# A new hand-written order for the VectorE, ScalarE and GpSimd steps and the output steps of a fused convolution, norm and gated FFN kernel

## The chip, the cores and the metric

The kernel runs on one core of a Trainium2 chip. The metric is the device time of one execution in microseconds (us). The kernel before takes 2584.48 us in the median of three runs (2583.52 to 2584.78).

The engines are named as in the profile: PE is TensorE's matmuls and PEld its weight loads, DVE is VectorE, ACT is ScalarE, POOL is GpSimd, and SP (SyncE) is used here for issuing DMAs.

## The reference

Two steps, from x of shape (8, 4096, 192), taken as 32768 tokens of 192 channels:

```python
# 1: causal depthwise convolution, 7 taps, one set of softmaxed taps for each of 8 heads of 24 channels
w = softmax(weight, axis=-1)                      # (8, 7)
y[b, s, c] = sum_k w[c // 24, k] * x_pad[b, s + k, c]      # x_pad: 6 zero rows in front of every batch
# 2: RMS norm and a gated FFN without biases
xn  = y / sqrt(mean(y * y, axis=-1) + 1e-6) * rms_g
g   = xn @ w_gate                                 # (32768, 1536)
val = xn @ w_val                                  # (32768, 1536)
out = (silu(g) * val) @ w_out                     # (32768, 192)
```

All arrays are f32 in DRAM.

## The kernel before, in words

**Pairs.** The 32768 tokens are worked on in 32 pairs of token tiles, a pair being two tiles of 512 tokens. Pair 0 is done plainly in the prologue, while the weights are converted. Pairs 1 to 31 all follow one list, `ORDER`, written out by hand; nothing at build time reorders it. A pair is a product stage and an output stage on TensorE. While TensorE works on pair p, the other engines also prepare pair p + 1 (its x operands), convolve pair p + 2, and finish pair p - 1 (a token of the list that ends in "-" belongs to the pair before).

**Fewer products.** Both matrix products go by a bilinear scheme: sums and differences of blocks of weights are made once, sums and differences of blocks of data in every pair, and then 15 products take the place of a larger number. The price is many elementwise sums, which is why VectorE, ScalarE and GpSimd are busy too.

**Product stage (L840).** The 1536 hidden columns are four units of 384. Each unit has 15 products, and each product is made twice: on the lower 64 rows of the TensorE array for the gate, on the upper 64 rows for the value, so a "round" is one product of each half. That is 4 x 15 x 2 = 120 products of 64x128 by 64x512 in a pair, in an order fixed by `CHAINS`. They land in eight PSUM banks of 512 columns, four for each half. A bank is free again only when another engine has read it, and the next product that takes it waits for that.

**The steps on a unit.** In the list, the first letter is the engine (A ScalarE, V or P or W VectorE, G GpSimd, Q an adding DMA issued by GpSimd's queue, D a DMA on SP's queue), and then comes the step: `AF0.1.0` is ScalarE doing step F0 for half 1 (upper) of unit 0. S copies a bank to a tile in SBUF, F copies a bank into another bank so that two sums can go on from it (L792 on ScalarE, L796 on VectorE), C, D and N (L866, L856, L860) combine a bank with a tile, R is a result (L874; with W it stays in its bank), G is the silu (L886, ScalarE), M multiplies gate and value (L894, VectorE or GpSimd). "p2" in the list means two TensorE steps. So a step's place in the list sets which TensorE steps it stands between, and its place in its own engine's queue; each engine takes its instructions strictly in that order, and the waits between engines come from the data.

**Sums of hidden columns.** From the hidden values (`ht`), sums such as `df`, `de`, `p4`, `ab`, `abe`, `abd`, `bcf` are made for the output stage, per unit: "Gde.2" is such a sum on GpSimd (L1074 for one unit, L1052 for several), "Qde.0" a DMA that adds one block to another in SBUF (L1050, L1072), and "Akp4.2 Pp4.2" a copy of one operand by ScalarE (L746) followed by the sum on VectorE. Units 0 to 3 have indices behind the dot, so "Qbe.0123" adds all four (1 MB), "Qabe.13" two of them (512 KB).

**Output stage (L1029).** 60 steps in the order of `OUTS`; "11.3" is output product 11 for unit 3. A step has four matmuls of 128x32 by 128x256, for four quarters. Each product number needs one of the sums above as its data. The accumulators use halves of PSUM banks, `BANKS` telling which; copies (F, S), joins (D, L1096), transposes (T, L1042) and the stores `st0`, `st1` (L1115, SP) take them to the output. Some of these steps for pair p run at the head of pair p + 1.

**The next pairs.** The convolution is 14 tap steps "cv k_j" per list (L471, L479) into halves of PSUM banks (`SIDE` says which). The norm is a square on ScalarE (`Asq`), a reduction, a power on GpSimd (L529) and a multiplication; `place` writes the result to DRAM (L687), and `fetA`, `fetB` (L703, L706) read it back as x operands. The x sums X0 to X6 and X22 (L738, L727; X22 makes two of them in one instruction) and the exchanges of array halves, `swA` and `swB` (L713, two DMAs each, on SP's queue), complete the operands of the next pair: x blocks are moved from the lower 64 partitions to the upper and back.

```python
nc.gpsimd.dma_start(out=dst, in_=b, accum_op=ALU.add)     # a Q step
```

The last pair has no pair behind it: `last()` puts its output steps in the order `LAST`, with the joins, transposes and stores as early as they can go.

Of the kernel before, what the change touches and what calls it, by code (L numbers as in the profile page):

```python
# [19 lines left out]
def kernel(  # L20
# [14 lines left out]
    H, K = weight.shape  # L35
# [53 lines left out]

    SPAN = 1509  # L90
    PLACE = {'a': 3, 'b': 4, 'c': 5, 'd': 0, 'e': 1, 'f': 2}
    BANKS = {'K': 1, 'R': 0, 'N': 0, 'C01': 0, 'C34': 1}
    OUTS = (
# [3 lines left out]
    )  # L97
    LAST = "7.2 14.2 10.1 13.0 13.2 13.3 13.1 12.0 12.3 12.2 12.1 3.0 0.3 0.0 0.1 0.2 2.0 2.1 2.3 2.2 1.1 1.2 1.3 1.0"
    ORDER = (
# [30 lines left out]
    )  # L130

    cst = ctx.enter_context(tc.tile_pool(name="cst", bufs=1))
# [330 lines left out]
    def part_tap(p, k, j):  # L463
# [4 lines left out]
        if k == 0:  # L468
            h = (SIDE if p > 2 else (0, 1, 0))[j]
            acc[p, j] = h, pick(h, False)  # L470
# [11 lines left out]
        if k == K - 1:  # L482
            h, i = acc.pop((p, j))
            free[h].append(i)
            ended[p] = ended.get(p, 0) + 1
            if ended[p] == len(SIDE):
                x_sb.pop(p)
# [280 lines left out]
    def pick(h, full):  # L768

        i = next((i for i in free[h] if ((h, i) in whole) == full), free[h][0])  # L770
        free[h].remove(i)
        return i
# [5 lines left out]
    def put(at, do):  # L778
        heapq.heappush(line, (at, next(tick), do))
# [148 lines left out]
            )  # L928
            yield

    SIDE = (1, 1, 1)
    regs = held[0 : 2 * NU] + [more[:, i] for i in range(2)]
    REG = {"AB": 0, "CB": 1, "X": 2, "S": 3}

# [26 lines left out]
    def out_steps(p):  # L961
        every, end = " ".join(OUTS).split(), LAST.split()
        return every if p < PAIRS - 1 else every[: -len(end)] + end

    class Pair:
# [29 lines left out]
        def open(self, b, full):  # L995
            b = PART.get(b, (b, 0))[0]
            if b in self.bk:
                return
            h = BANKS[b]
            i = pick(h, full)  # L1000
# [13 lines left out]
        def products(self):  # L1014
# [4 lines left out]
            for w in out_steps(self.p):  # L1019
                n, u = (int(i) for i in w.split("."))  # L1020
                src, b = LEFT[n]
                fresh = b in BANKS and b not in self.bk
                if fresh:
# [335 lines left out]

    for j in range(len(SIDE)):  # L1360
        put(c + 240 + 700 * (j // 2), functools.partial(part_tap, 2, 0, j))
# [152 lines left out]
```

## Time and profile before

| what | value |
|---|---|
| median of three runs | 2584.48 us |
| profiled execution | 2584.59 us, of which the span in the trace is 2582.8 |
| busy: PE, PEld, DVE, ACT, POOL | 99%, 63%, 93%, 76%, 80% of the span |
| granted TensorE clock | 0.999 of full speed |
| DMA | 259.33 MB, 100 GB/s in the mean |
| product stage, output stage of one pair | 52.98 us, 26.04 us |

The page is one profiled execution. Its first part gives for each engine the busy time, the share of the span and the number of instructions. The chain of waits starts from the last instruction and goes back, at each step to what released it, so its shares say what the end hung on. In a timeline, a row is start, duration, engine, line, operation, output and inputs by the program's names with partitions and elements, and in brackets the idle time of the engine before the row and what ended it. In the rows of groups, the number behind x is the count, then come busy time and the mean in ns. The DMA rows give the size of one and the median time from issue to landing.

### The profile page before, as it was taken

To read this page: it belongs to the slowest core of one execution; us is meant where nothing else is said; L and a number is where in the kernel's file an instruction comes from. 1 tells how busy PE (TensorE), PEld (TensorE's weight loads), DVE (VectorE), ACT (ScalarE), POOL (GpSimd) and SP (SyncE) were. 2 spreads that over 40 slices of the span, in tenths; PEclk is the share of its full clock that TensorE was granted. 3 is DMA by queue.
4 is the path that set the end of the run, shared out by engine and by line. 5 is a ranking of instruction groups with operands and counts; after the bars stand their busy time and mean duration, and the time that the engine had idled before them with its cause. 6 is when DMAs were issued, how large, how long until landed. Compare 5 with 4: busy or idle time off the path is not lost.

```text
span 2582.8 us, 61875 instructions
## 1 busy us (share of the span) xinstructions
PE 2568.2 (99%) x23114; PEld 1627.8 (63%) x23114; DVE 2405.7 (93%) x4009; ACT 1957.8 (76%) x3749; POOL 2056.9 (80%) x1581
## 2 busy tenths in 40 slices
PE   8999999999999999999999999999999999999999
PEld 6856666666666666666666666666666555666665
DVE  8799999999999999999999999999999999999976
ACT  6588777787777887777877778777788777787765
POOL 3897777977778877789777788777887777978777
PEclk9999999999999999999999999999999999999999
DMA  6444555445545545554455554455644455544442
GB/s 145 92 87 89 103 102 114 98 95 101 109 96 115 99 86 107 101 116 96 95 101 107 100 113 96 86 111 98 121 92 98 93 109 107 108 95 92 95 99 46
DMA packets 535411, 259.33 MB, mean 100 GB/s; under 512 B 458566, under 2 KB 462278, under 8 KB 531142
## 3 DMA queue, kind: packets, MB, share of 16 engines
q1 hardware_dynamic: 507316, 181.83, 34.7%
q0 software_dynamic: 26288, 73.15, 15.5%
q8 instruction: 182, 2.98, 0.5%
q14 instruction: 119, 0.97, 0.1%
q10 hardware_dynamic: 1506, 0.40, 0.1%
HBM read 100.10 MB, written 49.55 MB: 58 GB/s over the span
## 4 chain that ended last, share of the span: by engine, by line
PE 98%; ACT 1%; DMA 1%; POOL 0%; issue 0%; DVE 0%; SPq 0%; DVEq 0%; POOLq 0%; ACTq 0%
PE ps L840 63%; PE ps L1029 30%; PE ps L1161 2%; PE ps L1202 1%; DMA xa<-xa 0%; ACT early L412 0%; POOL xa L738 0%; DMA x<-in_x_dram 0%; POOL early L1052 0%; POOL early L1074 0%; ACT sq L597 0%; ACT xa L668 0%; PE ps L642 0%; ACT L434 0%; ACT tile L792 0%
## 5 line engine op out<-in xcount | busy, mean ns | idle before, releaser
L840 PE MATMUL ps<-xa,wf 64*128 64x512 f32 x7440 | 1646.4, 592 | 1.6 <-DMA xa<-xa 0.3
L840 PEld LDWEIGHTS ps<-xa,wf 64*128 64x128 f32 x7440 | 1050.0, 186 | 584.5 <-issue 122.8
L792 ACT ACTIVATE tile<-ps 128x512 f32<-128x512 f32 (+1 forms) x770 | 433.4, 570 | 199.5 <-PE ps L1029 108.3
L792 ACT ACTIVATE tls<-ps 128x512 f32<-128x512 f32 (+1 forms) x687 | 386.6, 567 | 167.8 <-PE ps L1029 103.5
L792 ACT ACTIVATE ps<-ps 128x512 f32<-128x512 f32 (+1 forms) x713 | 387.8, 547 | 122.0 <-PE ps L1029 92.0
L894 POOL TENSOR_TENSOR ht<-ht,tile 128x512 f32<-128x512 f32 x305 | 387.8, 1281 | 92.6 <-ACT tile L886 79.1
L1029 PE MATMUL ps<-ht,x 128*32 128x256 f32 x5952 | 390.6, 380 | 0.1
L894 POOL TENSOR_TENSOR ht<-ht,tls 128x512 f32<-128x512 f32 x253 | 321.8, 1279 | 63.6 <-ACT tls L886 55.2
L479 DVE SCALAR_TENSOR_TENSOR ps<-xh,tp,ps 128x512 f32<-128x512 f32 x450 | 322.8, 748 | 1.0 <-DMA xd<-yn 0.9
L1029 PEld LDWEIGHTS ps<-ht,x 128*32 128x32 f32 x5952 | 192.8, 110 | 143.8 <-issue 23.5
L1029 PE MATMUL ps<-early,x 128*32 128x256 f32 x3968 | 254.1, 379 | 0.0
L874 DVE TENSOR_TENSOR tile<-ps,tile 128x512 f32<-128x512 f32 x347 | 236.8, 685 | 15.0 <-ACT tile L792 7.7
L529 POOL TENSOR_TENSOR r<-r,nhalf 128x8 f32<-128x8 f32 x29 | 48.4, 1669 | 241.4 <-ACT r L525 241.4
L874 DVE TENSOR_TENSOR ht<-ps,tile 128x512 f32<-128x512 f32 x325 | 221.6, 685 | 10.4 <-ACT tile L792 6.3
L1052 POOL TENSOR_TENSOR early<-early,ht 128x1024 f32<-128x1024 f32 x93 | 225.9, 2496 | 0.7 <-PE ps L1029 0.2
L886 ACT ACTIVATE tile<-tile 128x512 f32<-128x512 f32 x347 | 215.7, 625 | 1.9
L874 DVE TENSOR_TENSOR tls<-ps,tls 128x512 f32<-128x512 f32 x273 | 185.4, 684 | 9.3 <-ACT tls L792 3.6
L1029 PEld LDWEIGHTS ps<-early,x 128*32 128x32 f32 x3968 | 129.6, 110 | 84.7 <-ACT ps L792 5.1
L886 ACT ACTIVATE tls<-tls 128x512 f32<-128x512 f32 x273 | 168.8, 624 | 1.7
L874 DVE TENSOR_TENSOR ht<-ps,tls 128x512 f32<-128x512 f32 x233 | 159.0, 684 | 6.1 <-ACT tls L792 3.4
L1074 POOL TENSOR_TENSOR early<-ht 128x512 f32<-128x512 f32 x124 | 159.6, 1287 | 2.7
L1029 PE MATMUL ps<-early,wo_sb 128*32 128x256 f32 x2232 | 143.6, 379 | 0.0
(165 smaller groups left out, 3629.1 us busy)
## 6 DMA issues: line engine op xcount, KB each, us to landing
xa<-xd SPq DMA_DIRECT2D x186, 256.0 KB, 4.4
xa<-xa SPq DMA_DIRECT2D x124, 256.0 KB, 4.0
ht<-ht POOLq DMA_DIRECT2D x31, 1024.0 KB, 7.7
xd<-yn SPq DMA_DIRECT2D x248, 96.0 KB, 2.5
out_dram<-o_sb SPq DMA_DIRECT2D x244, 96.0 KB, 2.0
xh<-in_x_dram SPq DMA_DIRECT2D x192, 105.0 KB, 3.7
xa<-xd SPq DMA_DIRECT2D x124, 128.0 KB, 4.8
more<-ht POOLq DMA_DIRECT2D x62, 256.0 KB, 3.3
```

The lines of the kernel that those rows point to most:

```text
L479: nc.vector.scalar_tensor_tensor(out=dst, in0=xk, scalar=w, in1=at, op0=ALU.mult, op1=ALU.add)
L529: nc.gpsimd.tensor_tensor(out=r, in0=r, in1=nhalf[:, 0 : nb * NR], op=ALU.pow)
L792: nc.scalar.activation(out=dst, in_=src, func=AF.Copy, scale=float(s))
L840: nc.tensor.matmul(out=self.new(v, h, True) if first else self.old(v, h), lhsT=wf[self.u][HALF[h], WAT[i], :], rhs=x_op(XOP[i], h), start= ...
L874: nc.vector.tensor_tensor(out=dst, in0=self.old(v, h), in1=t[:], op=plus(s))
L886: nc.scalar.activation(out=t[:], in_=src[:], func=AF.Silu)
L894: engine[eng].tensor_tensor(out=self.hv(v), in0=src, in1=t[:], op=ALU.mult)
L1029: nc.tensor.matmul(out=to[q * Q : (q + 1) * Q, :], lhsT=left[:, u, a], rhs=cols[:, i * HALFT : (i + 1) * HALFT], start=fresh, stop=True, s ...
L1052: nc.gpsimd.tensor_tensor(out=dst, in0=a, in1=b, op=ALU.add)
L1074: engine[eng].tensor_tensor(out=dst, in0=a, in1=b, op=ALU.add)
L1161: nc.tensor.matmul(out=bank(h, bks[h])[:], lhsT=wf[u][HALF[h], AT[h][k] * NF + f, :], rhs=xb[HALF[h], g, k, :], start=(k == 0), stop=(k == ...
L1202: nc.tensor.matmul(out=bank(h, bks[h])[:, w : w + D], lhsT=hts[f // NF][HALF[h], g, f % NF, j * P : (j + 1) * P], rhs=wo_sb[HALF[h], f, :] ...
```

## The change

The list `ORDER` is replaced by another order of nearly the same steps, and `OUTS`, `LAST`, one entry of `BANKS` and two of `SIDE` with it. The 180 TensorE steps of a pair and the number of steps on ScalarE (116), GpSimd (42 sums) and SP (8) in the list are the same; VectorE has one plain step fewer and one W step more (104 V, 15 P and 3 W for 105, 16 and 2), and there are four adding DMAs for five. What differs apart from places:

- copies of banks: `VF0.1.0` becomes `AF0.1.0`; `AF3.1.2` and `AF3.1.3` become `VF3.1.2` and `VF3.1.3`, while `VF3.0.2` and `VF3.0.3` become `AF3.0.2` and `AF3.0.3`
- products of gate and value: `GM2.1.3` becomes `VM2.1.3`, `GM3.1.2` becomes `VM3.1.2`, `VM5.1.3` becomes `GM5.1.3`; results kept in the bank are `WR3.1.2`, `WR2.1.3`, `WR3.1.3` instead of `WR3.1.3`, `WR5.1.3`
- adding DMAs: `Qde.0` and `Qde.1` become one `Qde.01`, `Qabe.13` becomes `Qabe.23` (with a new `Gabe.1` on GpSimd), `Qabd.0` becomes `Qabd.01`; `Qbe.0123` stays
- x sums: GpSimd's `GX5` and the two on VectorE `PX0` and `PX6` with their ScalarE copies become `GX0` and `GX22` on GpSimd
- the square of the norm (`Asq-`) is moved to the front of the pair
- the exchanges: `swA` from behind two TensorE steps of the next pair to four steps before the pair's end, `swB` from four steps before the end to five
- the stores `st0`, `st1` and the fetches `fetA`, `fetB` take other places in SP's queue
- one accumulator (`R`) opens in the other half of its bank, and so do two of the three groups of convolution taps (`SIDE`)

```diff
-    BANKS = {'K': 1, 'R': 0, 'N': 0, 'C01': 0, 'C34': 1}
+    BANKS = {'K': 1, 'R': 1, 'N': 0, 'C01': 0, 'C34': 1}
     OUTS = (
-        "6.2 11.2 6.0 6.1 11.0 11.1 6.3 4.0 11.3 4.1 4.2 9.1 14.0 14.3 14.1 4.3 9.2 9.0 9.3 8.1",
-        "8.3 5.0 5.2 5.1 5.3 8.0 3.1 7.0 8.2 10.2 7.1 10.0 3.3 3.2 10.3 7.3 7.2 14.2 10.1 13.0",
-        "1.1 13.2 1.2 12.0 12.3 12.2 12.1 13.3 13.1 3.0 1.3 1.0 0.3 0.0 0.1 2.0 0.2 2.1 2.3 2.2",
+        "6.0 11.1 11.2 4.0 6.3 11.0 6.2 6.1 11.3 4.2 4.1 14.2 14.3 14.1 14.0 9.1 4.3 9.2 9.0 9.3",
+        "8.1 8.2 8.3 8.0 5.1 5.3 5.2 3.0 5.0 13.1 3.3 10.0 13.0 7.2 3.1 7.3 3.2 7.0 7.1 10.2 1.1",
+        "1.2 12.3 1.3 10.3 10.1 12.1 13.3 12.2 12.0 1.0 13.2 0.3 0.0 2.0 2.1 2.3 0.2 2.2 0.1",
     )
...
     ORDER = (
-        "Vcv4_1- p2 VT2- DswA- VD1- Vcv5_1- VT4- Vcv6_1- p1 AS2- VT1- AS40.0.0 p1 VD2- VT0- VT5-",
-        "VD3- AS40.1.0 p1 AF0.0.0 Asq- p2 VT3- p1 VC.0.0 VF0.1.0 AS41.0.0 AS41.1.0 p1 VC.1.0 p2",
...
-        "Gp4.0 Dst0- AF2.1.2 p2 AG1.0.2 GM3.1.1 p2 AG0.0.2 VR0.1.2 VF3.0.2 VR2.0.2 AF3.1.2 p1",
-        "VR2.1.2 p1 AS44.0.2 p1 AG2.0.2 Qde.1 GM1.1.2 AS44.1.2 p3 AS40.0.3 VR5.0.2 GM0.1.2",
-        "VR5.1.2 p1 GM2.1.2 p1 VR3.0.2 AS40.1.3 VR3.1.2 AG4.0.2 p2 AF0.0.3 Gdf.2 p1 VM4.1.2",
...
-        "AF2.1.3 p1 AS44.0.3 p1 AG0.0.3 GM1.1.3 VF3.0.3 p1 VR5.0.3 AF3.1.3 p1 AS44.1.3 VR2.0.3",
-        "GM0.1.3 p1 DfetA VR2.1.3 VR3.0.3 AG2.0.3 GM2.1.3 WR3.1.3 Akp4.1 Pp4.1 p2 Gdf.3 AG5.0.3",
-        "Gde.3 WR5.1.3 Akp4.2 AG4.0.3 p3 Akcb.1 VM4.1.3 AG3.0.3 Akab.3 p1 Pcb.1 p2 Pp4.2 VM3.1.3",
...
-        "p2 PX3 DfetB Vcv6_2 p3 AkX1 Gbcf.3 p1 Akbcf.2 AS7 p1 AkX4 PX1 Acv0_1 p2 Pbcf.2 p3 Qabd.0",
-        "GX5 PX4 p1 VD7 p1 AkX6 AF4 p1 Vcv1_1 GX2 PX6 p2 Vcv2_1 p1 Gabd.13 AS13 p2 DswB p2 Gabd.2",
-        "p2 VD6 Vcv3_1 VD0 VD13",
+        "VD1- VD2- p1 Asq- p3 AS40.0.0 VT2- VD3- VT5- VT1- p1 AS40.1.0 AF0.0.0 p2 VT3- p1 VT4-",
+        "AF0.1.0 VC.0.0 p1 VC.1.0 AS41.0.0 p1 AS41.1.0 p1 Vred- AS00.0.0 Dst0- AS00.1.0 VD5.0.0",
...
+        "AG0.0.2 p1 VR0.1.2 AG1.0.2 VF3.1.2 VR2.0.2 VR2.1.2 p3 AS44.0.2 Gac.1 VR3.0.2 VR5.0.2",
+        "AS44.1.2 AG2.0.2 p2 VR5.1.2 WR3.1.2 p2 AG3.0.2 VM3.1.2 AS40.0.3 AS40.1.3 AG4.0.2 p1",
...
+        "AF3.0.3 Gde.2 p2 VR0.1.3 GM5.1.2 AS44.0.3 AG0.0.3 GM1.1.3 VF3.1.3 p1 GM0.1.3 VR5.0.3 p2",
+        "VR2.0.3 AS44.1.3 AG2.0.3 AG5.0.3 WR2.1.3 Akcb.2 p1 VR5.1.3 VM2.1.3 p3 Gcb.0 p2 VR3.0.3",
+        "p2 WR3.1.3 AG4.0.3 VM4.1.3 Akp4.2 Pp4.2 Gdf.3 Akp4.1 Pp4.1 Pcb.2 AG3.0.3 Akcb.3 Gde.3 p2",
...
+        "p1 Vcv5_0 Qabe.23 Pbce.2 Acv0_2 Vcv1_2 p3 Vcv2_2 AS5 AkX4 p2 PX4 Akbcf.1 AS6 Vcv6_0",
+        "Gbce.13 p1 Gbce.0 p1 Qabd.01 p1 Vcv3_2 p2 Pbcf.1 p2 AS7 Akbcf.2 p1 Gbcf.3 GX22 Vcv4_2",
+        "Gbcf.0 Acv0_1 p1 Vcv5_2 Pbcf.2 p9 Vcv1_1 Vcv6_2 AF4 p1 AS13 p2 GX2 Vcv2_1 Vcv3_1 VD0",
+        "Vcv4_1 DswB Gabd.3 p1 VD6 Gabd.2 Vcv5_1 DswA VD7 p1 Vcv6_1 VT0 p1 VD13 p2 AS2",
     )
...
-    SIDE = (1, 1, 1)
+    SIDE = (0, 1, 0)
```

More of the change, by code (lines that the diff above doesn't have):

```diff
@@ L91 @@
     PLACE = {'a': 3, 'b': 4, 'c': 5, 'd': 0, 'e': 1, 'f': 2}
-    BANKS = {'K': 1, 'R': 0, 'N': 0, 'C01': 0, 'C34': 1}
+    BANKS = {'K': 1, 'R': 1, 'N': 0, 'C01': 0, 'C34': 1}
     OUTS = (
[3 rows of a table removed]
[3 rows of a table added]
     )
-    LAST = "7.2 14.2 10.1 13.0 13.2 13.3 13.1 12.0 12.3 12.2 12.1 3.0 0.3 0.0 0.1 0.2 2.0 2.1 2.3 2.2 1.1 1.2 1.3 1.0"
+    LAST = "3.2 7.0 7.1 10.2 12.3 10.3 10.1 12.1 13.3 13.2 12.2 12.0 0.3 0.0 0.2 0.1 2.0 2.1 2.3 2.2 1.1 1.2 1.3 1.0"
     ORDER = (
[30 rows of a table removed]
[29 rows of a table added]
     )
```

37 rows, old and new, of the table ORDER are left out of this document.

## The prediction

> **What bounds the kernel now.** The page first: its engine line, then the chain by line.
>
> ```profile
> PE 2568.2 (99%) x23114; PEld 1627.8 (63%) x23114; DVE 2405.7 (93%) x4009; ACT 1957.8 (76%) x3749; POOL 2056.9 (80%) x1581
> ...
> PE 98%; ACT 1%; DMA 1%; POOL 0%; issue 0%; DVE 0%; SPq 0%; DVEq 0%; POOLq 0%; ACTq 0%
> ```
>
> TensorE sets the end, and at 99% seems to leave nothing. So I took the chain in order of time, to see whether it runs at its own pace.
>
> ```profile
> 677.30 50.96 PE ps L840 x234
> 730.28 26.04 PE ps L1029 x480
> ...
> 1859.52 5.39 DMA xa<-xa
> ```
>
> A pair of token tiles is a product stage (120 products on L840) and an output stage (60 steps, 480 records on L1029): 730.28 - 677.30 = 52.98 us, and 26.04. Their sum, 79.02, comes back 31 times; that is 2449.6 of the 2582.8. Now the same pair as a timeline, TensorE's weight loads among the others.
>
> ```profile
> 678.39 0.60 ACT L792 ACTIVATE tls<-ps 128x512 f32<-128x512 f32 x1 [0.64 <-PE ps L840]
> ...
> 680.18 0.69 DVE L866 TENSOR_TENSOR tls<-ps,tls 128x512 f32<-128x512 f32 x1 [0.47 <-PE ps L840]
> 680.34 0.19 PEld L840 LDWEIGHTS ps<-xa,wf 64*128 64x128 f32 x1 [0.24 <-issue]
> 680.77 0.19 PEld L840 LDWEIGHTS ps<-xa,wf 64*128 64x128 f32 x1 [0.24 <-issue]
> 680.79 0.69 DVE L796 COPY ps<-ps 128x512 f32<-128x512 f32 x1
> ...
> 681.38 0.68 DVE L866 TENSOR_TENSOR tile<-ps,tile 128x512 f32<-128x512 f32 x1
> 681.53 0.30 PEld L840 LDWEIGHTS ps<-xa,wf 64*128 64x128 f32 x4 [0.57 <-DVE ps L796]
> ...
> 728.30 0.30 PEld L840 LDWEIGHTS ps<-xa,wf 64*128 64x128 f32 x4 [0.86 <-ACT ps L792]
> ```
>
> Loads come 0.43 us apart, for the lower and the upper half of the array in turn, so each half takes a product every 0.86. At that pace 120 products take 51.5, and the stage takes 52.98: 1.46 is not product pace. Two loads come late: the tenth product of the pair waits for a Vector copy (0.57 idle where 0.24 is usual; from the load before it, 1.19 where 0.43 is due: 0.76), and one near the end for a Scalar copy (0.86 idle). I put 1.15 of the 1.46 on these two waits, both on the upper half, and 0.3 on the change of tile shape between the stages, which stays. So "99% busy" hides 1.15 us a pair, 35 us in all, and any wait of the new order is hidden in the same way. The Trainium skill (Perfetto Trace Analysis, Identifying the Most-Contended Engine) says that matmul busy time tells little of the distance to the limit because matmuls are pipelined, and to read the load's share instead; the trace agrees with the first half, while the load's 63% would promise a gain that 0.43 per product rules out.
>
> **The change part by part.** It is an order, so I compare what each hand-over to TensorE has of TensorE steps with what the instructions behind it take.
>
> *Loads of the engines.* Per pair VectorE has one 512-column step fewer (0.60), ScalarE the same number, GpSimd 42 sums as before and four adding DMAs for five. VectorE is busy 75 of 79 us, GpSimd 64, ScalarE 61: none becomes the bound by its sum.
>
> *The tenth product's copy* (VF0.1.0 becomes AF0.1.0). On VectorE it stood behind C (680.18) and ended at 681.48. On ScalarE it follows AF0.0.0, which in this timeline starts at 679.36; copies follow each other at 0.49, so it would run from 679.85 to 680.46, and the load is due at 680.34 + 0.43 = 680.77: 0.3 early. Of that the square (Asq, 1.48) takes some, since ScalarE now does it ahead of these copies; I leave 0.1. That wait goes. *The late Scalar copy* (AF3.1.3 becomes VF3.1.3, AF3.0.3 the other way) goes too: the two halves' copies now run side by side on two engines, where ScalarE did both in 2 x 0.5. Together 1.15 a pair.
>
> *What is late next in the product stage.* Product 46 of the upper half needs the bank that VR5.1.2 reads, and VR5.1.2 stands behind VR3.0.2 and VR5.0.2, which wait for product 43 of the lower half. From a load to the first reader of its product: 678.39 - 677.23 = 1.16. Then two Vector steps at 0.60 (680.18 to 680.79), one whole of 0.69, 0.05 to the load: 3.10. Three rounds of 0.86 and the 0.11 by which the halves are apart give 2.69. Late by 0.41. Smaller hand-overs of this kind add about 0.1. The product stage gains 1.15 - 0.5 = 0.65.
>
> *The output stage, first wait.* Step 11.3 needs Gdf.3 and Gde.3 on GpSimd, and they wait for the last column of unit 3, VM2.1.3, now VectorE's (was GM2.1.3). From product 56: 1.16, the copy AS44.1.3 0.63, four Vector steps 2.40, VM2.1.3 0.69, then Gdf.3 1.36, Gde.3 1.28 and 0.39 of hand-overs: 7.9. TensorE has four rounds of 0.86 less the half round that is done, the change of stage, and eight output steps of 0.434: 7.7. Late by 0.2; before, the sums of this step were just in time.
>
> *Second wait.* Step 12.0 needs Gbcf.0, and GpSimd's order is Qabd.01, Gbcf.3, GX22, Gbcf.0, where Gbcf.3 waits for step 7.3. These rows price it:
>
> ```profile
> L1074 POOL TENSOR_TENSOR early<-ht 128x512 f32<-128x512 f32 x124 | 159.6, 1287 | 2.7
> ...
> L1074 POOL TENSOR_TENSOR early<-early,ht 128x512 f32<-128x512 f32 x93 | 129.9, 1397 | 0.0
> ...
> L738 POOL TENSOR_TENSOR xa<-xa 128x512 f32<-128x512 f32 x65 | 96.4, 1722 | 1.4 <-DMA xa<-xd 1.3
> ```
>
> A sum right behind an adding DMA takes 1.72 (L738), others 1.29 to 1.40; the double sum X22 was seen once, 2.36 (L727, in the prologue). Step 7.3 to GpSimd 0.50, Gbcf.3 1.72, X22 2.36, Gbcf.0 1.29, back to a load 0.31: 6.18 with little overlap. Fourteen steps of 0.434 less the last one's drain give 5.86. Late by 0.3 (0 with Gbcf.3 at 1.29; 0.6 with 2.5 for X22, as the two-unit sums of L1052 take, and 1.4 for Gbcf.0). Both waits cost 0.5. With 0.05 for hand-overs that have under 0.15 to spare (the new order has more of these in the output stage), a pair gains 0.65 - 0.5 - 0.05 = 0.1, and 30 pairs 3.0 us.
>
> *Adding DMAs.*
>
> ```profile
> ht<-ht POOLq DMA_DIRECT2D x31, 1024.0 KB, 7.7
> ...
> more<-ht POOLq DMA_DIRECT2D x62, 256.0 KB, 3.3
> early<-ht POOLq DMA_DIRECT2D x31, 512.0 KB, 8.4
> ```
>
> Qde.01 has over 11 us. Qabe.23 is issued 3.8 us behind the 1 MB add, where the 512 KB add of before was 2.7 behind; by that row it lands about 7.3 after issue, and 13.3 asks for it after 9.7. Qabd.01, 512 KB where 256 was, has step 13.0 to step 2.0, 21 steps or 9.1 us, less 0.5 to issue: 8.6, of which 0.3 is the load's. It lands between 3.3 (256 KB) and 8.4 (512 KB, but queued behind the 1 MB); alone, a line through 3.3 and 7.7 gives 4.8, the nearer row, so it costs nothing; the upper end costs 0.1 to 0.3 a pair. Adds of 256 KB landed after 3.3 to 3.6 in the median with VectorE 93% busy. The Trainium skill (SBUF — State Buffer, SBUF: two separate sides) warns that a VectorE copy within SBUF can lock GpSimd out, so that a DMA issued there starves for descriptors; its section on a bandwidth pool gives 620 ns grown to 3100. By an estimate of 2.5 us more from that figure Qabd.01 would still be in time at 4.8, and 2.5 a pair late at 8.4, 2655 in all; the 3.3 speaks against it, and I give it none of the chance.
>
> *Exchanges.* The two on SP (L713) move: swA from after two products of the next pair to four output steps before the end, swB one step earlier, both ahead of SP's loads and stores, which have slack of many us. An exchange lands after 4.0 (3.2 to 6.2). Before, a few were late: the chain passes one at 1859.52, and that pair takes 1917.21 - 1837.77 = 79.44; three such cost 1.4 us. With a microsecond more they go: 1.4.
>
> *The two ends.* The prologue is the same, and the last output steps and the closing stores keep their order: nothing, within 2 us either way.
>
> Sum: 2584.6 (the profiled execution; its span is 2582.8, and the median of the runs 2584.5, 0.1 less) - 3.0 - 1.4 = 2580, or -0.2%. 0.2%, 5.2 us, is about what a measurement of this kernel can tell from no change.
>
> **The rivals.** *Faster, output waits absent.* If GpSimd's sums run at 1.29 and VM2.1.3 is ready earlier, the 0.5 falls away: 30 x 0.6 + 1.4 = 19 us, 2565; half of it, 2573. For it: 1.29 is the commoner row. Against: both chains are long, and each link can only add. *Slower, GpSimd's slow sums.* If its sums before the two waits run at the slow rows (1.40 for a single sum, 2.5 for a double), the first wait grows from 0.2 to 0.4 (Gdf.3 and Gde.3, 0.1 each) and the second from 0.3 to 0.6; a pair loses 0.4 + 0.6 + 0.05 - 0.65 = 0.4, and 30 x 0.4 - 1.4 = 10.6, 2595. It decides once the two waits together pass 0.60 + (5.2 + 1.4) / 30 = 0.82. For it: L1074's 1.40 on just these tiles. Against: those 1.40s follow a DMA or a double sum only. A late Qabd.01 alone adds 30 x 0.3 = 9 to the sum: 2589. *The order does nothing that it is for.* If the exchanges were late as before, because their inputs come no earlier, 1.4 stays: 2581.5, still within 0.2%.
>
> **How the numbers follow.** About even 0.39 (the sum and the third rival, 2579.4 to 2589.8, its own range 2579 to 2587), faster 0.36, slower 0.25 (0.18 GpSimd, 0.07 the add together with waits that I don't see). The predicted time is that of the even case, 2580. Eight in ten lie between 2566, short of the whole gain, and 2594, short of the whole loss.
>
> **What would show it.** Right: no wait of loads on DVE ps L796, the product stage at 52.3 instead of 52.98, the output stage at 26.5, waits of loads on L1029 for POOL early and POOL nt of 0.2 to 0.4 once a pair, and no exchange in the chain. Wrong: an output stage at 26.0 (faster) or at 26.8 and more (slower), a load waiting for DMA early<-ht, or a product stage that stays near 53.

## The result, and the profile after

The changed kernel takes 2565.28 us in the median of four runs (2565.09 to 2565.88), the kernel before 2584.16 (2583.52 to 2584.78). The ratio is 0.9927, with a 95% interval of 0.991 to 0.9945: 19 us or 0.7% faster. The forecast was 2580 in a range of 2566 to 2594, so the time fell just out of the range, on the fast side, where the first rival stood (2565, "output waits absent").

The engine line and the chain by line of the changed kernel:

```profile
PE 2550.2 (99%) x23114; PEld 1742.0 (68%) x23114; DVE 2380.5 (93%) x3980; ACT 1955.1 (76%) x3751; POOL 1976.3 (77%) x1549
...
PE 99%; ACT 0%; DVE 0%; ACTq 0%; issue 0%; DVEq 0%
```

They say as little as before: 99% and 99%. The chain in order of time (start, duration, work) shows the difference. L839 is now the product stage, L1028 the output stage (all lines behind the lists moved up by one):

```profile
672.97 52.35 PE ps L839 x239
725.32 26.11 PE ps L1028 x480
751.42 52.35 PE ps L839 x239
```

A product stage takes 52.35 where it took 52.98, an output stage 26.11 where it took 26.04. The product stage is what the prediction forecast (52.3); the output stage is not (26.5). No exchange of array halves is left in the chain.

The weight loads at the start of the pair that begins at 751.42 (start, duration, and in brackets the idle time before the row and what ended it):

```profile
753.17 1.48 PEld L839 LDWEIGHTS ps<-xa,wf 64*128 64x128 f32 x8 [0.24 <-issue]
754.89 5.66 PEld L839 LDWEIGHTS ps<-xa,wf 64*128 64x128 f32 x27 [0.24 <-issue]
760.87 1.58 PEld L839 LDWEIGHTS ps<-xa,wf 64*128 64x128 f32 x9 [0.32 <-ACT ps L791]
```

The wait of 0.57 for a Vector copy is gone: from 753.17 on no load is idle for longer than 0.32, where 0.24 is usual. The wait near the end of the stage is gone too. The output stage has the first of the two waits that the prediction named:

```profile
806.11 0.78 PEld L1028 LDWEIGHTS ps<-ht,x 128*32 128x32 f32 x16
807.23 0.16 PEld L1028 LDWEIGHTS ps<-nt,x 128*32 128x32 f32 x8 [0.35 <-POOL nt L1073]
807.48 0.35 PEld L1028 LDWEIGHTS ps<-tls,wo_sb 128*32 128x32 f32 x8
807.91 0.35 PEld L1028 LDWEIGHTS ps<-early,wo_sb 128*32 128x32 f32 x8
```

The row of 806.11 holds two steps, 0.43 apart, so step 11.3 (the row of 807.23) was due at 806.97 and its load comes 0.26 late. But the next one is due another 0.43 later, at 807.41, and comes at 807.48: only 0.07 is left of it. The second wait, for Gbcf.0, isn't seen in the rows of the loads at all. GpSimd's rows show why:

```profile
819.01 0.84 POOL L1049 DMA_DIRECT2D early<-ht  x1
819.72 1.45 POOL L1073 TENSOR_TENSOR early<-early,ht 128x512 f32<-128x512 f32 x1
820.97 2.54 POOL L726 TENSOR_TENSOR xa<-xa 128x1024 f32<-128x1024 f32 x1
823.31 1.42 POOL L1073 TENSOR_TENSOR early<-early,ht 128x512 f32<-128x512 f32 x1
```

Gbcf.3 is recorded with 1.45, but X22 starts 1.25 behind its start; X22 is recorded with 2.54, and Gbcf.0 starts 2.34 behind (1.25 and 2.34 are the medians of all pairs too). Recorded durations on GpSimd overlap here; the starts count.

### The profile page after: what moved, and what is told of

Read it like the earlier page. It is cut to its first block, busy times and chain, and to the rows that moved or that the text cites. A ratio compares the mean times of both kernels' runs of the same rounds, so it can differ in the third digit from the quotient of the medians.

```text
span 2563.4 us, 61935 instructions
## 1 busy us (share of the span) xinstructions
PE 2550.2 (99%) x23114; PEld 1742.0 (68%) x23114; DVE 2380.5 (93%) x3980; ACT 1955.1 (76%) x3751; POOL 1976.3 (77%) x1549
## 4 chain that ended last, share of the span: by engine, by line
PE 99%; ACT 0%; DVE 0%; ACTq 0%; issue 0%; DVEq 0%
PE ps L839 63%; PE ps L1028 32%; PE ps L1160 3%; PE ps L1201 1%; PE ps L415 0%; PE ps L581 0%; ACT sq L596 0%; ACT xa L667 0%; PE ps L641 0%; ACTq L265 0%; ACT L277 0%; ACT tile L791 0%; DVE ps L1095 0%; DVE o_sb L1041 0%; DVE y L437 0%
## 5 line engine op out<-in xcount | busy, mean ns | idle before, releaser
L839 PE MATMUL ps<-xa,wf 64*128 64x512 f32 x7440 | 1625.5, 591 | 0.0
L839 PEld LDWEIGHTS ps<-xa,wf 64*128 64x128 f32 x7440 | 1172.1, 187 | 439.9 <-issue 104.5
L791 ACT ACTIVATE tile<-ps 128x512 f32<-128x512 f32 (+1 forms) x817 | 449.4, 568 | 159.7 <-PE ps L1028 88.6
L791 ACT ACTIVATE ps<-ps 128x512 f32<-128x512 f32 x744 | 403.4, 548 | 173.5 <-PE ps L1028 123.5
L791 ACT ACTIVATE tls<-ps 128x512 f32<-128x512 f32 (+1 forms) x640 | 355.6, 569 | 106.7 <-PE ps L1028 48.2
L1028 PE MATMUL ps<-ht,x 128*32 128x256 f32 x5952 | 401.1, 380 | 0.5 <-ACT ps L791 0.5
L893 POOL TENSOR_TENSOR ht<-ht,tls 128x512 f32<-128x512 f32 x230 | 292.9, 1276 | 106.5 <-ACT tls L885 105.7
L478 DVE SCALAR_TENSOR_TENSOR ps<-xh,tp,ps 128x512 f32<-128x512 f32 x450 | 337.1, 751 | 6.2 <-DMA xd<-yn 0.9
L1028 PEld LDWEIGHTS ps<-ht,x 128*32 128x32 f32 x5952 | 189.9, 110 | 146.9 <-POOL ht L893 23.5
L1073 POOL TENSOR_TENSOR early<-early,ht 128x512 f32<-128x512 f32 x186 | 250.4, 1375 | 7.3 <-PE ps L1028 4.1
L1028 PE MATMUL ps<-early,x 128*32 128x256 f32 x3968 | 253.7, 379 | 0.0
L873 DVE TENSOR_TENSOR tile<-ps,tile 128x512 f32<-128x512 f32 x344 | 233.8, 686 | 19.3 <-PE ps L839 11.2
L873 DVE TENSOR_TENSOR ht<-ps,tile 128x512 f32<-128x512 f32 x300 | 203.4, 681 | 0.0
L1028 PEld LDWEIGHTS ps<-early,x 128*32 128x32 f32 x3968 | 129.2, 110 | 84.9
L745 ACT COPY ps<-ht 128x512 f32<-128x512 f32 x217 | 127.2, 586 | 62.9 <-DVE xa L737 42.3
L1028 PE MATMUL ps<-early,wo_sb 128*32 128x256 f32 x2232 | 154.6, 379 | 0.2 <-ACT tile L791 0.2
```

What stands on the lines that cost most here:

```text
L478: nc.vector.scalar_tensor_tensor(out=dst, in0=xk, scalar=w, in1=at, op0=ALU.mult, op1=ALU.add)
L745: nc.scalar.copy(out=bank(*at)[:], in_=src)
L791: nc.scalar.activation(out=dst, in_=src, func=AF.Copy, scale=float(s))
L839: nc.tensor.matmul(out=self.new(v, h, True) if first else self.old(v, h), lhsT=wf[self.u][HALF[h], WAT[i], :], rhs=x_op(XOP[i], h), start= ...
L873: nc.vector.tensor_tensor(out=dst, in0=self.old(v, h), in1=t[:], op=plus(s))
L893: engine[eng].tensor_tensor(out=self.hv(v), in0=src, in1=t[:], op=ALU.mult)
```

## The experiments

Three things are told apart: what the two removed waits of the product stage are worth, each and together; why the output stage did not pay; and where the late exchanges went. All times are medians, and ratios are to runs of the kernel before on the same chip at the same time (2584.38 for the runs that change steps, 2584.55 for the square and the small sums).

### The tenth product's copy back on VectorE

```diff
-        "AF0.1.0 VC.0.0 p1 VC.1.0 AS41.0.0 ...
+        "VC.0.0 VF0.1.0 p1 VC.1.0 AS41.0.0 ...
```

> The changed kernel with its copy for the tenth product back on VectorE and behind C (VF0.1.0 for AF0.1.0). Theory 'each wait its own price' (the prediction's): the load of that product is about 0.76 us late again and every pair pays it, 30 x 0.76 = 23 us, about 2588, product stage 53.1. Theory 'one chain for each half of the array': a half pays only what a wait adds to the delay that it already has. The upper half of the changed kernel collects 0.55 a pair in small pieces behind this place (loads late by up to 0.42); with 0.76 in front, those pieces are covered. Product stage 52.35 + 0.1 to 0.2, total 3 to 6 us more, 2568 to 2571.

Measured: 2570.24 (0.9945 of before, 0.9931 to 0.996), 5 us more than the changed kernel. The chain, and the load that waits:

```profile
673.77 52.56 PE ps L839 x240
726.33 26.04 PE ps L1028 x480
```

```profile
755.84 0.19 PEld L839 LDWEIGHTS ps<-xa,wf 64*128 64x128 f32 x1 [0.24 <-issue]
756.60 0.30 PEld L839 LDWEIGHTS ps<-xa,wf 64*128 64x128 f32 x4 [0.57 <-DVE ps L795]
```

The old wait is back, with its 0.57. The stage grows by 0.21 alone. In the starts of the matmuls 0.44 is paid for this wait, and of the three small waits that the changed kernel has behind this place (0.08, 0.10 and 0.06) none is left: 0.44 - 0.23 = 0.21. The output stage is at 26.04 again. Its load for step 11.3 still waits for GpSimd:

```profile
729.69 0.18 PEld L1028 LDWEIGHTS ps<-nt,x 128*32 128x32 f32 x8 [0.25 <-POOL nt L1073]
```

But it is only 0.17 late (0.25 idle where 0.09 is usual), and that costs nothing; the small sums below show why. So a wait does not have its own price: where TensorE waits early, what it would have waited for later has time to get done. The total fits the theory of one chain, at the upper end of what it gave.

### Both copies back

```diff
-        "AF3.0.3 Gde.2 p2 VR0.1.3 GM5.1.2 AS44.0.3 AG0.0.3 GM1.1.3 VF3.1.3 p1 ...
+        "VF3.0.3 Gde.2 p2 VR0.1.3 GM5.1.2 AS44.0.3 AG0.0.3 GM1.1.3 AF3.1.3 p1 ...
```

and the edit above.

> The changed kernel with both copies as they were before: VF0.1.0, and the forks of unit 3 as VF3.0.3 and AF3.1.3. 'Each wait its own price': 0.76 and 0.39 on top of the 0.55 that stays: 30 x 1.15 = 34 us, about 2600, product stage 53.5. 'One chain for each half': 0.76 first, then a load that is 0.74 late of which 0.42 exceeds the delay so far: 1.18 in place of 0.55, product stage back at 52.97, total 30 x 0.62 = 19 us more, 2584.

Measured: 2583.42 (0.9997, 0.9987 to 1.0006). Output stages in the chain, 79.02 apart:

```profile
967.40 26.04 PE ps L1028 x480
1046.42 26.04 PE ps L1028 x480
```

79.02 - 26.04 = 52.98: with two copies undone, and all the rest of the new order left in place, a pair takes what it took before. Without these two copies nothing of the gain is left. They do not add up from single parts, though: the first alone takes back 0.14 a pair (78.46 to 78.60), the second, on top of it, 0.42. No run undoes the second alone in the changed kernel, so how the 0.56 would split in the other order stays open.

### The tenth product's copy alone, in the kernel before

```diff
-        "VD3- AS40.1.0 p1 AF0.0.0 Asq- p2 VT3- p1 VC.0.0 VF0.1.0 AS41.0.0 ...
+        "VD3- AS40.1.0 p1 AF0.0.0 p2 VT3- AF0.1.0 Asq- p1 VC.0.0 AS41.0.0 ...
```

> The kernel before with one step changed: the tenth product's copy on ScalarE, ahead of the square, which follows it at once (AF0.1.0 Asq in place of Asq and VF0.1.0). 'Each wait its own price': 0.76 a pair is gone, 30 x 0.76 = 23 us, 2561. 'One chain for each half': the square (1.48) now stands in front of the next copies on ScalarE, whose loads become late by some 0.4, and the late fork near the end (0.74 late) finds less delay to hide behind: the stage stays within 0.1 of 52.98, total within 3 us of 2584.

Measured: 2582.96 (0.9994, 0.9985 to 1.0004): no change that can be told. A stretch of its chain, in which one output stage starts where the product stage before it ends, 651.22 - 598.29 = 52.93:

```profile
572.25 26.04 PE ps L1029 x480
598.29 50.92 PE ps L840 x231
651.22 26.04 PE ps L1029 x480
```

The copy that is worth a wait of 0.57 brings 0.05 a pair by itself. In the starts of the matmuls the wait at the tenth product is gone, and small ones of 0.02 to 0.10, 0.25 together, stand at rounds 8 to 15 instead; the late fork near the end, which cost 0.42 before, now costs 0.56. The total came out as the theory of one chain had it, but not for the reason that it gave: the last pair has no square (the last square starts at 2419, that pair's first product at 2495), and its product stage takes 52.93 all the same, with 0.25 of small waits at rounds 12 to 15 and 0.56 at the fork. So it is not the square that keeps this copy from paying here.

### The square back in front of the copy

```diff
-        "VD1- VD2- p1 Asq- p3 AS40.0.0 VT2- ... AF0.0.0 p2 VT3- ...
+        "VD1- VD2- p4 AS40.0.0 VT2- ... AF0.0.0 Asq- p2 VT3- ...
```

> The changed kernel with the norm's square (1.48 us on ScalarE) back between AF0.0.0 and AF0.1.0, where it stood before. The tenth product's load is late by about 1.1 us. 'Each wait its own price': 30 x 1.1 = 33 us, 2598. 'One chain for each half of the array': 1.1 in place of the 0.55 that the upper half collects in the changed kernel: 0.55 a pair, 17 us, 2582, product stage 52.9. Either way the earlier square carries most of what the new copy brings.

Measured: 2587.07 (1.001, 1.0 to 1.0019), 22 us more than the changed kernel; 17 was expected with one chain for each half, 33 with a price for each wait. The load of the tenth product:

```profile
761.01 0.19 PEld L839 LDWEIGHTS ps<-xa,wf 64*128 64x128 f32 x1 [0.24 <-issue]
762.39 0.30 PEld L839 LDWEIGHTS ps<-xa,wf 64*128 64x128 f32 x4 [1.20 <-ACT ps L791]
```

In the starts of the matmuls 1.06 is paid there, about the 1.1 that I had put down. The small waits behind it are gone again, but they are 0.23 in the starts of the changed kernel, and not the 0.55 that the theory of one chain took off: 1.06 - 0.23 = 0.83. The product stage is 53.18, 0.83 longer, and the output stage 0.07 shorter: 0.76 x 30 = 23. So the place of the square, which the prediction mentions in half a sentence, carries the copy: with the square where it was, the new order would be no faster than the old one. The run holds its own control. Its last square starts at 2424, in the pair before the last, and the product stage of the last pair, without one, takes what it takes in the changed kernel (where the last pair takes what the others take):

```profile
2500.38 52.35 PE ps L839 x239
```

### What a late load costs in the output stage

Small sums that nothing uses, ahead of Gbcf.0 on GpSimd, one and four of them:

```diff
-        "Gbcf.0 Acv0_1 p1 Vcv5_2 ...
+        "Gz1 Gbcf.0 Acv0_1 p1 Vcv5_2 ...      # Gz4 in the second kernel
...
+            elif act[0] == "z":
+                for _ in range(int(act[1:])):
+                    nc.gpsimd.tensor_tensor(
+                        out=own[:, 0:3], in0=own[:, 3:6], in1=own[:, 3:6], op=ALU.add
+                    )
```

> The changed kernel with one small extra sum (128x24, not used by anything) on GpSimd right ahead of Gbcf.0, for which step 12.0 waits. From the rows of 128x256 (0.725) and 128x512 (1.275) such a sum is estimated at 0.2. If a late load is paid in full (the prediction's pricing), the output stage grows by 0.2 a pair: 26.3, 6 us in all, 2571. If a load of the output stage may come late by the 0.2 that it is ahead of its matmul, of which 0.05 is used up now: by 0.05 at most, total within 2 us of 2565.3.

> The same with four such sums, about 0.8 us. Paid in full: output stage 26.9, 24 us, 2589. With the load's head start: 0.8 less 0.17, output stage 26.7, 19 us, 2584; the difference between four sums and one is then three whole sums, while the first costs nearly nothing.

Measured: 2566.48 with one (0.993, 0.9915 to 0.9945), 2593.54 with four (1.0035, 1.0022 to 1.0048). GpSimd's rows, first with one sum:

```profile
823.40 0.36 POOL L1120 TENSOR_TENSOR own<-own 128x24 f32<-128x24 f32 x1
823.58 1.41 POOL L1073 TENSOR_TENSOR early<-early,ht 128x512 f32<-128x512 f32 x1
```

then with four:

```profile
990.79 1.28 POOL L1120 TENSOR_TENSOR own<-own 128x24 f32<-128x24 f32 x4
992.03 1.27 POOL L1073 TENSOR_TENSOR early<-early,ht 128x512 f32<-128x512 f32 x1
```

One sum puts Gbcf.0 off by 0.18, and the output stage goes from 26.11 to 26.14: 0.03 is paid. Four put it off by 1.24 (I had estimated 0.8; in the trace each of them waits for the one before), and the stage goes to 27.05: 0.94 is paid. The starts say how. With nothing in the way, a load of the output stage starts 0.21 to 0.22 before its matmul, as here in the changed kernel, for the step ahead of 12.0 and 12.0 itself:

```profile
824.31 0.78 PEld L1028 LDWEIGHTS ps<-early,wo_sb 128*32 128x32 f32 x16
824.53 1.05 PE L1028 MATMUL ps<-early,wo_sb 128*32 128x256 f32 x16
```

With four sums the load of step 12.0 and its matmul start together:

```profile
993.36 0.16 PEld L1028 LDWEIGHTS ps<-early,wo_sb 128*32 128x32 f32 x8 [1.22 <-POOL early L1073]
993.36 0.64 PE L1028 MATMUL ps<-early,wo_sb 128*32 128x256 f32 x8 [0.74 <-POOL early L1073]
```

The load is 1.14 late, and its matmul 0.92 late, against the same step where it waits for nothing (the next kernel). So a load of this stage may be late by 0.21 for nothing. In the changed kernel the load of 12.0 starts right behind the end of Gbcf.0 (0.05), and its matmul is on time. So GpSimd's chain does end at the edge, as the prediction had it, but inside that 0.21; whatever is added to it beyond that is paid in full.

### X22 behind Gbcf.0

```diff
-        ... Akbcf.2 p1 Gbcf.3 GX22 Vcv4_2",
-        "Gbcf.0 Acv0_1 p1 Vcv5_2 ...
+        ... Akbcf.2 p1 Gbcf.3 Vcv4_2",
+        "Gbcf.0 GX22 Acv0_1 p1 Vcv5_2 ...
```

> The changed kernel with X22 moved behind Gbcf.0 on GpSimd, so that Gbcf.0 is ready 2.3 us sooner and the exchange that needs X22 starts about 1.25 us later. If step 12.0 pays 0.3 a pair for GpSimd's chain (the prediction): 30 x 0.3 = 9 us less, 2556, output stage 25.8. If that chain is just in time in the changed kernel: output stage stays at 26.11, no gain; and if it was X22's early sum, and not the place of the exchange in the list, that ended the late exchanges, some pairs wait for an exchange again, 1 to 3 us more, 2566 to 2568.

Measured: 2565.45 (0.9927, 0.9912 to 0.9942), the same as the changed kernel. With 2.3 us taken out of the chain ahead of step 12.0 the output stage stays at 26.10: there was nothing to gain, which settles the second wait from the other side. It also moves the exchanges later. The rows of SP's queue show when the first of them is issued: in the changed kernel 6.3 us ahead of the next pair's first load (829.82), in this one 5.0 ahead of it (829.53), as in the kernel before.

```profile
823.53 3.81 SPq L712 DMA_DIRECT2D xa<-xa  x4
```

```profile
824.50 3.29 SPq L712 DMA_DIRECT2D xa<-xa  x4
```

In this kernel one pair of 30 waits for an exchange, 0.53 us; in the changed kernel, none; in the kernel before, five, 1.7 us together. The exchange is released by X22 or, before, by PX6, and not by its place in the list: in both kernels here the first of them is issued 0.03 behind the end of X22 in every pair, and before it is issued at 751.27, 0.07 behind the end of PX6. This speaks for X22's earlier sum as what ended the late exchanges. The other five changed kernels, in which X22 stays ahead of Gbcf.0, have none behind their first pair either, but one late pair in one profile on the other side is thin, and I leave it at that.

## Why the prediction was wrong, by its own steps

**The product stage: right in its number, in part by luck.** Gain 0.65 a pair forecast, 0.63 measured; 52.3 forecast, 52.35 measured. The waits that go and the ones that come were named rightly, but both parts were priced too high by about the same amount. In the starts of the matmuls the two removed waits cost 0.435 and 0.419, together 0.85 and not 1.15; the new ones cost 0.08, 0.10 and 0.06, together 0.23 and not 0.5. VR5.1.2, which I put at 0.41, is the 0.10. In the first of the old waits 0.76 was priced and 0.44 is paid, in this new one 0.41 and 0.10: 0.3 too much in both, which cancels in the difference without a reason that the prediction gave. The excess of the stage over 51.5 that stays is 0.62 without any wait, and not the 0.3 that I set aside for the change of shape. And the parts are not independent, as the single edits show: only their sum over this order is 0.62.

**The output stage, first wait: the step that failed, in its size.** 0.2 late forecast, 0.26 late measured, but 0.07 paid; 0.17 late, with the tenth product's copy back on VectorE, costs nothing. I priced the lateness of a load as lateness of TensorE.

**The output stage, second wait: the step that failed most.** 0.3 forecast, nothing paid. Two things were off. "Gbcf.3 1.72" took a recorded duration, and laid it to the adding DMA ahead; that reading of L738 was wrong. In the kernel before (748.68, two sums in 2.99) both of its sums are recorded with 1.75, only the first stands behind an adding DMA, and they start 1.24 apart; the sum of L1074 behind an adding DMA is recorded with 1.44. In the changed kernel the next instruction starts 1.25 behind Gbcf.3. With starts, the sum is 0.50 + 1.25 + 2.34 + 1.42 + 0.31 = 5.82 against 5.86, in time; the page's durations made 6.18 of it. And what would be left over is covered by the load's 0.21. The chain itself, Gbcf.3, X22, Gbcf.0 ahead of step 12.0, is there as forecast, and four small sums in it cost 28 us; in the changed kernel it just doesn't end last.

**Other hand-overs, 0.05:** no price for them is left, since the 0.07 stands behind step 11.3. In all, the output stage costs 0.07 where 0.55 was forecast, and this 0.48 a pair, 14 us, is nearly the whole miss of 15.

**Adding DMAs: right.**

```profile
early<-ht POOLq DMA_DIRECT2D x62, 512.0 KB, 6.9
more<-ht POOLq DMA_DIRECT2D x31, 512.0 KB, 4.6
```

The two adds into `early` land after 6.9 in the median; taken singly, Qabe.23 after 7.5 (7.3 forecast) and Qabd.01 after 5.4 (4.8 forecast, in time up to 8.3). Qde.01, alone, lands after 4.6. No load of pairs 1 to 31 waits for one. With VectorE 93% busy, no starving of the adding DMAs is seen. The Trainium skill (SBUF — State Buffer, SBUF: two separate sides) warns of that for a VectorE copy within SBUF. VectorE's copies and 512-column sums in these pairs read or write a PSUM bank (`ps`), so these pairs don't put the warning to the test.

**Exchanges: about right in size** (1.4 forecast, 1.7 in the kernel before and none after; three pairs at 79.44 - 79.02 = 0.42 make 1.3, and there were five late ones). The reason is probably another one than forecast: the first of them is earlier because X22, the sum that it waits for, is earlier, and not because its issue moved in the list.

**The ends:** the first product stage is 1.76 shorter, not 0.63, and the prologue and the last output stage with the closing stores together are 1.15 longer: 0.6 in all, within the 2 us given.

**Sum.** With one figure more, a pair gains 0.626 - 0.075; 30 x 0.55 = 16.5, 1.7 for exchanges and some 0.5 for other late pairs of before, 0.6 for the ends: 19.3. The spans differ by 19.4.

**The chances.** "Output waits absent" had 0.36 and was priced at 2565. Its ground, that 1.29 is the commoner row, was near the truth, and the argument against it, "each link can only add", was not: links overlap. The range ended one microsecond short of it, because I took that case as too complete.

## What to carry to other kernels

Add up distances from start to start, not recorded durations: on GpSimd the two differ here by 0.2 to 0.5 us for one sum. Price the lateness of a matmul, not of its weight load; a load that waits may cost nothing (up to 0.21 late in this output stage). And where several waits lie in one stage, undo them singly and together before giving each a price: here one of them was worth 0.05 or 0.14 alone, and the two together all of the gain.

## What was not expected

- The same wait, 0.57 idle before one load, stands in two kernels whose product stages differ by 0.42 (52.98 and 52.56).
- A small sum of 128x24 on GpSimd costs 0.18 from start to start where it comes alone, and four in a row, each waiting for the one before, 1.24, for their recorded 0.36 and 1.28.
- How the two halves of the array share a wait was not measured by itself: the theory of one chain for each half gave the total of three of the four product-stage runs within 2 us, but with the square back it took off 0.55 of small waits where the starts show 0.23, and for the copy alone in the kernel before its reason did not hold. The starts of the two halves alternate in the record, and no run separated them.
